# Row sums beside the output, and the last weight piece as two requests, in an attention and soft-MoE kernel

## The chip, the cores and the metric

The kernel runs on one core of a Trainium2 chip. The metric is the device time of one execution in microseconds (us). Five engines work side by side, each through its own queue in order: PE (TensorE: matmuls; PEld, its weight loads, overlap them), DVE (VectorE), ACT (ScalarE), POOL (GpSimd) and SP (SyncE, which here only issues transfers). The data itself is moved by 16 DMA engines. PE writes its results to PSUM, and ACT and DVE evict them to SBUF.

## What is computed

Causal attention with 16 extra "beacon" keys in front gives tokens x, and a soft mixture of experts runs over all tokens. In the reference, cut to what matters:

```python
x = attn_out.transpose(0, 2, 1, 3).reshape(B * S, H * D)      # 4608 x 512
logits = x @ phi                                              # 4608 x 32 slots
d = np.exp(logits - logits.max(0)); d /= d.sum(0) + 1e-09     # over the tokens
slot_input = (d.T @ x).reshape(E, S_per_e, D)                 # 8 experts, 4 slots each
for e in range(E):
    slot_out[e] = np.maximum(slot_input[e] @ w1[e], 0.0) @ w2[e]
c = np.exp(logits - logits.max(1)); c /= c.sum(1) + 1e-09     # over the slots
return c @ slot_out                                           # 4608 x 512
```

B = 8 batches, H = 8 heads, S = 576 tokens, D = 64; w1 is 8 x 512 x 1024, w2 8 x 1024 x 512. No maximum is subtracted in the kernel's fast path: exp of the logits is taken as it is, and a range test at the end, the flag, decides whether a general path has to run after it.

## The kernel before

**Attention.** The main loop (L746 to L783) runs over 32 pairs of heads. For each it computes scores, exponentials, the weighted values and the normalization, and, a few pairs later, transposes x, computes logits and adds each batch's share to the slot inputs (`dispatch`). The exponentials of the logits, transposed, are kept in `eT` (128 x 4608, f16): the 32 slots' rows stand four times over, one below the other. The order of work on every engine is the order in which the program writes it (`manual_schedule`, L666).

**Weights.** `load_weights` (L442) takes 512 KB pieces (f16 as stored; f32 is read and cast on the way) from the list `wchunks` and issues each from POOL's queue. The last in the list is expert 7's second-layer weight, second half (chunks c = 4 to 7), in a tile named `wt`. L786 issues what is left, after the memset of `siz`.

**The tail (L789 to L867).** The last pair is finished, the last batch's logits and slot inputs are computed; `fill` puts in dummy matmuls between them. Then follow `first(eg, fh)` (first layer of four experts at once, half of its 1024 columns), `turn(eg)` (transposes of the result), and `second(eg, c0, c1)` (second layer; it loops over chunks c, inside over four experts, and accumulates in the PSUM tile `so`). `so1` (L863) is its eviction, scaled.

**Row sums.** The output of a token has to be divided by the sum of its 32 exponentials. `row_sums(bb)` (L659) does nine matmuls of `row_tokens(bb, j)` with a column of ones; bb counts quarters of the 4608 tokens (each 128 x 9; two batches of the reference), called batches below. `row_factors` (L840) adds 1e-9 into `stat` and writes the reciprocals into `rc`, on DVE. All four batches' sums share one PSUM tile with `so` (`rsps`). The order on PE is: sums of batch 0 ahead of the last `dispatch`, batch 1 ahead of `first(0, 0)`, batch 2 ahead of `second(1)`, batch 3 behind so1; the factors of 0 and 1 follow `first(0, 0)`, those of 2 and 3 follow the sums of 3 (L865, L866).

**Output (L869 to L924).** For each batch and each j a matmul (L911, tile `fps`, six PSUM buffers) gives 128 x 512 outputs, evicted alternately by ACT (L916) and DVE (L918), scaled by `rc`, into `osb`; SP issues the transfers (L922), three j at a time (six buffers); the first batch begins with one j, then two. The very first j is evicted in two halves, by ACT and DVE at once.

**Range test.** POOL runs three tests of three instructions each (L884 to L888): of `stat` (all sums, 357 columns), of `so1` and of the slot inputs `sz1`. `judge` (L891), called behind the third batch, takes minima on DVE, a matmul, and writes the flag.

Of the kernel before, what the change touches and what calls it, by code (L numbers as in the profile page):

```python
# [9 lines left out]
FP = mybir.dt.float32  # L10
# [3 lines left out]
AL = mybir.AluOpType  # L14
# [37 lines left out]
NJ = 9  # L52
# [3 lines left out]
SUM_LO = 8.0  # L56
SUM_HI = 60000.0
# [211 lines left out]
def kernel(  # L269
# [12 lines left out]
    nc = tc.nc  # L282
    P = 128
    B, H, S, D = q.shape
    Nb = beacon_k.shape[2]
    E, Dm, F = moe_w1.shape
    NSL = moe_phi.shape[1]
    SPE = NSL // E
    NDC = Dm // P
# [16 lines left out]
    ones32 = const.tile([P, 1], F16, name="ones32")  # L306
# [9 lines left out]
    sz1 = const.tile([P, NDC * NSL], F16, name="sz1")  # L316
# [5 lines left out]
    NST = NPAIR * 2 * NC5  # L322
    stat = const.tile([P, NST + 36 + 1], FP, name="stat")

    rd = const.tile([P, 1], FP, name="rd")
    rc = const.tile([P, 4, NJ], FP, name="rc")
    so1 = const.tile([P, Dm], F16, name="so1")
# [6 lines left out]
    ps_av = es.enter_context(tc.tile_pool(name="ps_av", bufs=1, space=PSUM))  # L334
    ps_tr = es.enter_context(tc.tile_pool(name="ps_tr", bufs=2, space=PSUM))
# [60 lines left out]
    def perm_v(b):  # L396
# [12 lines left out]
        for i in range(2):  # L409
# [4 lines left out]
    wchunks = [(e, m, j) for es_ in ((0, 1, 2, 3), (4,)) for m in range(2)  # L414
               for e in es_ for j in range(2)]
    wchunks += [(e, 0, j) for e in (5, 6, 7) for j in range(2)]
    wchunks += [(e, 1, j) for j in range(2) for e in (5, 6, 7)]
    wtail = {}

    def piece(e, m, j):  # L420

        if e < NRES:
            if m == 0:
                return w1h[e][:, 2 * j:2 * j + 2, :].rearrange("p t f -> p (t f)")
            return w2h[e][:, 4 * j:4 * j + 4, :].rearrange("p c d -> p (c d)")
        if (e, m, j) not in wtail:
            if e == NRES:
                t = stv.tile([P, 2, 2048], F16, name="wv", tag="v", bufs=2)
                for i in range(2):
                    wtail[e, m, i] = t[:, i, :]  # L430
            else:
                t = stq.tile([P, 2048], F16, name="wt", tag="kq"[len(wtail) % 2])
                wtail[e, m, j] = t[:, :]
        return wtail[e, m, j]
# [7 lines left out]
    def load_weights(count):  # L442
        for _ in range(count):
            if not wchunks:
                return
            e, m, j = wchunks.pop(0)
            if m == 0:
                nc.gpsimd.dma_start(
                    out=piece(e, m, j),
                    in_=moe_w1[e, 2 * j * P:2 * (j + 1) * P, :].rearrange("(p t) f -> p (t f)", t=2))  # L450
            else:
                src = moe_w2[e].rearrange("(p c) d -> p c d", c=NFC)
                nc.gpsimd.dma_start(
                    out=piece(e, m, j),
                    in_=src[:, 4 * j:4 * j + 4, :].rearrange("p c d -> p (c d)"))

    qTs = {}

# [187 lines left out]
    def row_tokens(bb, j):  # L646

        return eT[:, 2 * S * bb:2 * S * (bb + 1)].rearrange("s (p j) -> s j p", j=NJ)[:, j, :]

    def fill(count, late=True):  # L650

        pool, tag = (ps_tr, "tr") if late else (ps_av, "av")
        ps = pool.tile([P, 512], FP, name="fill", tag=tag)
        for _ in range(count):
            nc.tensor.matmul(ps[:, :], onesh[:, :], eT[:, 0:512], start=True, stop=True)  # L655

    rsp = {}

    def row_sums(bb):  # L659
        if bb == 0:  # L660
            rsp[0] = ps_av.tile([P, 2, 512], FP, name="rsps", tag="av")
        for j in range(NJ):
            nc.tensor.matmul(rsp[0][:, 1, bb * NJ + j:bb * NJ + j + 1], row_tokens(bb, j),
                             ones32[:, :], start=True, stop=True)

    with tc.manual_schedule(engines={ET.PE, ET.DVE, ET.Activation, ET.Pool, ET.SP}):  # L666
        load_qk(0, 0, first=True)
# [2 lines left out]
                          in_=beacon_k.rearrange("b h n d -> (b h) (n d)"))  # L670
# [44 lines left out]
        for c in range(4):  # L715
            for t in range(4):
                nc.vector.tensor_copy(
                    out=sel[32 * c:32 * c + 32, t, :].rearrange(
                        "p (m t) -> p m t", t=4)[:, :, t],
                    in_=idh[32 * c:32 * c + 32, 32 * c:32 * c + 32])  # L720
# [25 lines left out]
        for n in range(2, NPAIR):  # L746
            b, g = divmod(n, NG)
# [46 lines left out]
        normalize(n - 1)  # L794
        x_transposes(n - 2)
        dispatch(B - 2)
        fill(1)
        x_transposes(n - 1)
        logits(B - 1, 0, NDC - 1)
        logits(B - 1, NDC - 1, NDC)  # L800
        row_sums(0)
        sp = dispatch(B - 1, sizv)
        nc.gpsimd.tensor_copy(
            out=sz1[:, :].rearrange("p (t e s) -> p t e s", t=NDC, s=SPE), in_=sizv)
# [29 lines left out]
                        start=(eg == 0 and c == 0),  # L834
                        stop=(eg == E // 4 - 1 and c == NFC - 1))

        rsv = stat[:, NST:NST + 36]
        rcf = rc[:, :, :].rearrange("p a j -> p (a j)")

        def row_factors(j0, j1):  # L840
            nc.vector.tensor_scalar(out=rsv[:, j0:j1], in0=rsp[0][:, 1, j0:j1], scalar1=1e-9,  # L841
                                    scalar2=None, op0=AL.add)
            nc.vector.reciprocal(out=rcf[:, j0:j1], in_=rsv[:, j0:j1])

        row_sums(1)
        first(0, 0)
        row_factors(0, 2 * NJ)
        first(0, 1)
        slot_sums(B - 1, sp, sizv)
        nc.vector.tensor_scalar(out=rd[:, :], in0=stat[:, NST + 36:], scalar1=0.0625e-9,  # L850
                                scalar2=None, op0=AL.add)
# [2 lines left out]
        turn(0)  # L854
        first(1, 1)
        combine_T(B - 1)
        so = rsp[0][:, 0, :]
        second(0, 0, NFC // 2)
        turn(1)
        second(0, NFC // 2)  # L860
        row_sums(2)
        second(1)
        nc.vector.tensor_scalar(out=so1[:, :], in0=so, scalar1=rd[:, 0:1], scalar2=None,  # L863
                                op0=AL.mult)
        row_sums(3)  # L865
        row_factors(2 * NJ, 4 * NJ)  # L866
        es.close()  # L867

        m3 = fast.enter_context(tc.tile_pool(name="m3", bufs=6))  # L869
# [5 lines left out]
        ps_g = fast.enter_context(tc.tile_pool(name="ps_g", bufs=1, space=PSUM))  # L875
# [1 line left out]
        gm = gd.tile([P, 1], FP, name="gm")  # L877
        goodh = gd.tile([P, 1], F16, name="goodh")
        tests = []
        for src, w, low in ((stat, NST + 36 + 1, SUM_LO), (so1, Dm, -SUM_HI),  # L880
                            (sz1, NDC * NSL, -SUM_HI)):
            lo = gd.tile([P, w], FP, name="lo", tag=f"lo{w}")
            hi = gd.tile([P, w], FP, name="hi", tag=f"hi{w}")
            nc.gpsimd.tensor_scalar(out=lo[:, :], in0=src[:, :], scalar1=low, scalar2=None,  # L884
                                    op0=AL.is_ge)
            nc.gpsimd.tensor_scalar(out=hi[:, :], in0=src[:, :], scalar1=SUM_HI, scalar2=None,
                                    op0=AL.is_le)
            nc.gpsimd.tensor_tensor(out=lo[:, :], in0=lo[:, :], in1=hi[:, :], op=AL.mult)  # L888
            tests.append(lo)

        def judge():  # L891
            for i, lo in enumerate(tests):
                nc.vector.tensor_reduce(out=good[:, i:i + 1], in_=lo[:, :], axis=AX.X, op=AL.min)
            nc.vector.tensor_tensor(out=gm[:, :], in0=good[:, 0:1], in1=good[:, 1:2], op=AL.mult)
            nc.vector.tensor_tensor(out=goodh[:, :], in0=gm[:, :], in1=good[:, 2:3], op=AL.mult)
            gp_ = ps_g.tile([1, 1], FP, name="gps")
            nc.tensor.matmul(gp_[:, :], goodh[:, :], onesh[:, 0:1], start=True, stop=True)
            nc.vector.tensor_scalar(out=flag[:, :], in0=gp_[:, :], scalar1=P - 0.5, scalar2=None,
                                    op0=AL.is_lt)
# [3 lines left out]
        for bb in range(4):  # L903
            for (j0, j1) in JS if bb else [(0, 1), (1, 3)] + JS[1:]:
                osb = m3.tile([P, 3, Dm], FP, name="osb", tag="osb")
                for j in range(j0, j1):
                    hw = Dm // 2 if cnt == 0 else Dm
                    fp_ = [ps_f.tile([P, Dm], FP, name="fps", tag="fps")
                           for _ in range(Dm // hw)]
                    for i, f in enumerate(fp_):  # L910
                        nc.tensor.matmul(f[:, 0:hw], row_tokens(bb, j),  # L911
                                         so1[:, hw * i:hw * i + hw], start=True, stop=True)
                    for i, f in enumerate(fp_):
                        ou = osb[:, j - j0, hw * i:hw * i + hw]
                        if (cnt + i) % 2 == 0:
                            nc.scalar.activation(ou, f[:, 0:hw], AF.Copy, scale=rc[:, bb, j:j + 1])  # L916
                        else:
                            nc.vector.tensor_scalar(out=ou, in0=f[:, 0:hw],  # L918
                                                    scalar1=rc[:, bb, j:j + 1], scalar2=None,
                                                    op0=AL.mult)  # L920
                    cnt += 1
                nc.sync.dma_start(out=outr[bb, :, j0:j1, :], in_=osb[:, 0:j1 - j0, :])  # L922
            if bb == 2:
                judge()  # L924
    fast.close()
# [34 lines left out]
```

## Time and profile before

| what | value |
|---|---|
| median of 3 runs (lowest, highest) | 203.09 us (202.74, 204.77) |
| the profiled execution's own time | 203.09 us |
| its span, first to last instruction | 201.4 us |
| busy: PE, DVE, ACT, POOL | 163.2, 132.2, 133.9, 113.9 us |
| moved by the 16 DMA engines | 55.90 MB, mean 278 GB/s |
| mean granted TensorE clock | 0.950 |

How to read the lines further below. On the page, each digit of an engine's line is its busy share, in tenths, of one of 40 equal slices of the span; a queue's line gives packets, MB and the share of 16 engines' span that its packets took. A line of the chain of waits or of the timeline starts with start and length in us; then come the engine, the tile or the operation, and the line of the program; in brackets stands how long the engine had been idle, and what ended that. "SPq", "POOLq" and "DVEq" are those engines' sequencers. A line of a stretch gives its bounds and length, then the busy time (and instructions) of PE, PEld, DVE, ACT and POOL, the granted PE clock, the DMA share and GB/s.

### The profile page before, as it was taken

How to read it: one execution, taken by the hardware profiler on the slowest of the kernel's cores; microseconds unless marked ns; L12 is line 12 of the kernel's file. 1: busy time of each engine (PE TensorE's matmuls, PEld its weight loads, DVE VectorE, ACT ScalarE, POOL GpSimd, SP SyncE). 2: the span in 40 equal slices, each digit the busy share in tenths (PEclk: the TensorE clock that was granted, in tenths of full speed). 3: DMA queues.
4: the chain of work that ended last, by engine and by line, in shares of the span. 5: the costliest groups of instructions: out<-in, count | busy, mean ns of one | idle time of the engine just before them, and what ended most of it. 6: DMA issues, size and time to landing. Idle time of an engine off the chain costs nothing.

```text
span 201.4 us, 7361 instructions
## 1 busy us (share of the span) xinstructions
PE 163.2 (81%) x3121; PEld 107.9 (54%) x3121; DVE 132.2 (66%) x275; ACT 133.9 (66%) x172; POOL 113.9 (57%) x263
## 2 busy tenths in 40 slices
PE   6798893889889898988988899898989997966200
PEld 2433661668567476666756667675767753522000
DVE  0352784688987888887887878878837332898300
ACT  2355784689878888889887788987895230774200
POOL 6049186469649757865965786898786000890000
PEclk9999999799999999999999999999999999995855
DMA  6999999999999999999999999999999991499991
GB/s 206 254 244 365 278 361 317 270 370 311 267 271 378 264 261 349 292 275 305 356 232 279 379 273 268 264 219 217 211 216 212 213 202 30 176 410 417 408 405 78
DMA packets 29701, 55.90 MB, mean 278 GB/s; under 512 B 7228, under 2 KB 15644, under 8 KB 29660
## 3 DMA queue, kind: packets, MB, share of 16 engines
q1 hardware_dynamic: 24764, 37.98, 55.4%
q0 software_dynamic: 4608, 16.78, 41.7%
q10 hardware_dynamic: 288, 0.59, 1.0%
q8 instruction: 26, 0.43, 0.8%
q14 instruction: 15, 0.12, 0.2%
HBM read 62.69 MB, written 9.44 MB: 358 GB/s over the span
## 4 chain that ended last, share of the span: by engine, by line
PE 60%; DMA 10%; ACT 9%; DVE 8%; POOL 3%; issue 3%; SPq 0%; ACTq 0%; DVEq 0%; POOLq 0%
PE sc L514 15%; PE av L535 15%; PE trps L483 9%; DMA wt<-in_moe_w_dram 7%; ACT expT L519 5%; PE xtps L561 5%; DVE osb L918 4%; ACT vh L407 4%; PE vpt L404 2%; DMA kstag<-in_k_dram 2%; PE fill L655 2%; PE fps L911 2%; PE lgps L580 2%; PE vps L404 2%; PE sips L619 2%
## 5 line engine op out<-in xcount | busy, mean ns | idle before, releaser
L519 ACT ACTIVATE expT<-sc 128x992 f16<-128x992 f32 (+3 forms) x128 | 104.8, 867 | 20.6 <-PE sc L514 20.0
L505 POOL TENSOR_SCALAR_AFFINE_SELECT expT<-expT 128x224 f16<-128x224 f16 (+3 forms) x128 | 54.9, 439 | 40.1 <-ACT expT L519 39.2
L514 PE MATMUL sc<-qT,kT 64*128 64x80 bf16 (+4 forms) x576 | 43.8, 246 | 10.8 <-ACT expT L519 5.5
L535 PE MATMUL av<-vh,expT 128*128 128x65 f16 (+1 forms) x960 | 40.4, 195 | 0.4 <-DVE x L549 0.2
L535 PEld LDWEIGHTS <-expT 128*128 128x128 f16 (+1 forms) x960 | 33.7, 98 | 4.5 <-POOL expT L505 0.6
L495 DVE COPY kT<-trps 128x640 bf16<-128x640 bf16 (+1 forms) x31 | 22.7, 773 | 19.8 <-PE trps L483 19.3
L514 PEld LDWEIGHTS <-kT 64*128 64x128 bf16 x576 | 17.0, 95 | 28.1 <-issue 22.2
L495 DVE COPY qT<-trps 128x640 bf16<-128x640 bf16 (+1 forms) x30 | 22.0, 774 | 8.2 <-PE trps L483 6.3
L549 DVE TENSOR_TENSOR x<-av,r 128x640 f16<-128x640 f32 x32 | 26.4, 825 | 1.1
L390 POOL CAST vc<-vstag 128x512 f16<-128x512 f32 x32 | 18.6, 611 | 1.8 <-DMA vstag<-in_beacon_v_dram 1.8
L916 ACT ACTIVATE osb<-fps,rc 128x512 f32<-128x512 f32 (+1 forms) x18 | 11.0, 678 | 12.2 <-PE fps L911 10.9
L568 DVE COPY xT<-xtps 128x576 f16<-128x576 f16 x31 | 14.2, 457 | 6.5 <-PE xtps L561 6.5
L561 PE MATMUL xtps<-idh,x 128*128 128x128 f16 (+2 forms) x160 | 14.1, 216 | 1.1 <-issue 1.0
L918 DVE TENSOR_SCALAR osb<-fps,rc 128x512 f32<-128x512 f32 (+1 forms) x19 | 12.8, 731 | 1.3 <-PE fps L911 1.1
L655 PE MATMUL fill<-eT,onesh 128*128 128x512 f16 x35 | 11.4, 453 | 1.7 <-POOL onesh L684 1.5
L407 ACT ACTIVATE vh<-vps 128x1024 f16<-128x1024 f32 x8 | 8.2, 1027 | 6.6 <-PE vpt L404 6.6
L561 PEld LDWEIGHTS <-x 128*128 128x128 f16 (+2 forms) x160 | 9.0, 97 | 6.6 <-issue 6.0
L410 DVE CAST vh<-vpt 128x512 f16<-128x512 f32 x16 | 10.3, 685 | 3.4 <-PE vpt L404 3.4
L911 PE MATMUL fps<-so,eT 128*128 128x512 f16 (+1 forms) x37 | 11.6, 433 | 0.5 <-DVE stat L841 0.3
L462 POOL COPY kT<-bkA 64x32 bf16<-64x32 bf16 x32 | 7.4, 231 | 7.9 <-DVE bkA L712 6.9
L483 PE MATMUL trps<-idb,kstag 128*64 128x128 bf16 x270 | 11.6, 234 | 0.1
L483 PE MATMUL trps<-idb,qstag 128*64 128x128 bf16 x270 | 10.7, 222 | 0.5 <-DVE vh L410 0.4
(98 smaller groups left out, 186.7 us busy)
## 6 DMA issues: line engine op xcount, KB each, us to landing
kstag<-in_k_dram SPq DMA_DIRECT2D x15, 576.0 KB, 9.4
qstag<-in_q_dram SPq DMA_DIRECT2D x15, 576.0 KB, 13.4
out_dram<-osb SPq DMA_DIRECT2D x11, 768.0 KB, 7.6
vstag<-in_v_dram SPq DMA_DIRECT2D x7, 1024.0 KB, 15.3
w1h<-in_moe_w_dram POOLq DMA_DIRECT2D x10, 512.0 KB, 8.6
w2h<-in_moe_w_dram POOLq DMA_DIRECT2D x10, 512.0 KB, 8.5
wt<-in_moe_w_dram POOLq DMA_DIRECT2D x8, 512.0 KB, 12.2
wv<-in_moe_w_dram POOLq DMA_DIRECT2D x4, 512.0 KB, 11.6
```

Of the source, the lines that this page charges most:

```text
L390: nc.gpsimd.tensor_copy(out=st["c", b][:, :, hs, :].rearrange("p t h d -> p h t d"), in_=st["v", b][:, hs, :, :])
L407: nc.scalar.activation(vhs[b % 2][:, 0:2, :, 0:D], ps[:, :, :].rearrange("p c (h d) -> p c h d", d=D), AF.Copy)
L483: nc.tensor.transpose(tp[lo:hi, j - j0, :], t[:, hh, j, :].bitcast(BF)[:, 1::2], idb[:, :])
L495: nc.vector.tensor_copy(out=do, in_=ti)
L505: nc.gpsimd.affine_select(out=ap, in_=ap, compare_op=AL.is_ge, fill=0.0, base=cbase, pattern=pat, channel_multiplier=-1)
L514: nc.tensor.matmul(sc[:, hh, col:col + qw], kTs[n // 2 % 2][po:po + D, n % 2, c * P:(c + 1) * P], qTs[n // 2][po:po + D, n % 2, q0:q0 + qw ...
L519: nc.scalar.activation(ex[:, :, base:base + w], sc[:, :, 0:w], AF.Exp, scale=scale)
L535: nc.tensor.matmul(av[:, i, :], exps[n % 2][0:KW[c], hh, o:o + P], vhs[b % 2][0:KW[c], c, h, :], start=(c == 0), stop=(c == i))
L549: nc.vector.tensor_tensor(out=xs[b][:, :, head(n, 0):head(n, 1) + 1:head(n, 1) - head(n, 0), :].rearrange("p i h d -> p h i d"), in0=av[:, ...
L561: nc.tensor.transpose(tp[:, QLO[i]:QLO[i] + QW[i]], xs[b][0:QW[i], i, 2 * t:2 * t + 2, :].rearrange("p h d -> p (h d)"), idh[0:QW[i], 0:QW ...
L911: nc.tensor.matmul(f[:, 0:hw], row_tokens(bb, j), so1[:, hw * i:hw * i + hw], start=True, stop=True)
L918: nc.vector.tensor_scalar(out=ou, in0=f[:, 0:hw], scalar1=rc[:, bb, j:j + 1], scalar2=None, op0=AL.mult)
```

## The change

Four edits go together. (1) The last weight piece is issued as two requests of two chunks each. (2) `row_sums` gets its PSUM tile as an argument and does the factors itself, for one batch; batch 0's tile comes from the pool of transposes, batch 1's from that of `av`, and `so` has a tile of its own. (3) The sums of batches 2 and 3 move into the output loop, behind the third request of batch 0 and the second request of batch 1 (j = 3 to 5), with a PSUM tile of the one-buffer pool that the judge's matmul uses too. (4) The test of `stat` moves from the head of POOL's tests into `judge`, so POOL tests `so1` and `sz1` first. A second dummy matmul is added ahead of the last x transposes.

```diff
+    WLAST = wchunks[-1]
...
-                nc.gpsimd.dma_start(
-                    out=piece(e, m, j),
-                    in_=src[:, 4 * j:4 * j + 4, :].rearrange("p c d -> p (c d)"))
+                cs = 2 if (e, m, j) == WLAST else 4
+                for c in range(0, 4, cs):
+                    nc.gpsimd.dma_start(
+                        out=piece(e, m, j)[:, c * Dm:(c + cs) * Dm],
+                        in_=src[:, 4 * j + c:4 * j + c + cs, :].rearrange("p c d -> p (c d)"))
...
-    rsp = {}
-
-    def row_sums(bb):
-        if bb == 0:
-            rsp[0] = ps_av.tile([P, 2, 512], FP, name="rsps", tag="av")
+    rsv = stat[:, NST:NST + 36]
+    rcf = rc[:, :, :].rearrange("p a j -> p (a j)")
+
+    def row_sums(bb, rsp):
+
         for j in range(NJ):
-            nc.tensor.matmul(rsp[0][:, 1, bb * NJ + j:bb * NJ + j + 1], row_tokens(bb, j),
-                             ones32[:, :], start=True, stop=True)
+            nc.tensor.matmul(rsp[:, j:j + 1], row_tokens(bb, j), ones32[:, :], start=True,
+                             stop=True)
+        sl = slice(bb * NJ, bb * NJ + NJ)
+        nc.vector.tensor_scalar(out=rsv[:, sl], in0=rsp[:, 0:NJ], scalar1=1e-9, scalar2=None,
+                                op0=AL.add)
+        nc.vector.reciprocal(out=rcf[:, sl], in_=rsv[:, sl])
...
-        fill(1)
+        fill(2)
...
-        row_sums(0)
+        row_sums(0, ps_tr.tile([P, NJ], FP, name="rsps", tag="tr"))
...
-        row_sums(1)
+        row_sums(1, ps_av.tile([P, 2, 512], FP, name="rsps", tag="av")[:, 0, :])
         first(0, 0)
-        row_factors(0, 2 * NJ)
         first(0, 1)
...
-        so = rsp[0][:, 0, :]
+        so = ps_av.tile([P, 2, 512], FP, name="so", tag="av")[:, 0, :]
         second(0, 0, NFC // 2)
         turn(1)
         second(0, NFC // 2)
-        row_sums(2)
         second(1)
         nc.vector.tensor_scalar(out=so1[:, :], in0=so, scalar1=rd[:, 0:1], scalar2=None,
                                 op0=AL.mult)
-        row_sums(3)
-        row_factors(2 * NJ, 4 * NJ)
...
+        test(so1, Dm, -SUM_HI)
+        test(sz1, NDC * NSL, -SUM_HI)
+
         def judge():
+            test(stat, NST + 36 + 1, SUM_LO)
...
                 nc.sync.dma_start(out=outr[bb, :, j0:j1, :], in_=osb[:, 0:j1 - j0, :])
+                if bb in (0, 1) and j0 == 3:
+                    row_sums(bb + 2, ps_g.tile([P, NJ], FP, name="rsps", tag="g"))
             if bb == 2:
                 judge()
```

More of the change, by code (lines that the diff above doesn't have):

```diff
@@ L835, in second @@
                         stop=(eg == E // 4 - 1 and c == NFC - 1))
[L837 to L843, printed above, removed]
-        row_sums(1)
+        row_sums(1, ps_av.tile([P, 2, 512], FP, name="rsps", tag="av")[:, 0, :])
         first(0, 0)
-        row_factors(0, 2 * NJ)
         first(0, 1)
@@ L879, with test @@
         tests = []
-        for src, w, low in ((stat, NST + 36 + 1, SUM_LO), (so1, Dm, -SUM_HI),
-                            (sz1, NDC * NSL, -SUM_HI)):
+        def test(src, w, low):
             lo = gd.tile([P, w], FP, name="lo", tag=f"lo{w}")
@@ L895, in judge @@
             nc.vector.tensor_tensor(out=goodh[:, :], in0=gm[:, :], in1=good[:, 2:3], op=AL.mult)
-            gp_ = ps_g.tile([1, 1], FP, name="gps")
+            gp_ = ps_g.tile([1, 1], FP, name="gps", tag="g")
             nc.tensor.matmul(gp_[:, :], goodh[:, :], onesh[:, 0:1], start=True, stop=True)
```

## The prediction, made before the result was known

> **What bounds the kernel now.** I read the page first, then the chain of waits, then the transfers second by second around the place where the weights end and the output begins.
>
> ```profile
> span 201.4 us, 7361 instructions
> PE 163.2 (81%) x3121; PEld 107.9 (54%) x3121; DVE 132.2 (66%) x275; ACT 133.9 (66%) x172; POOL 113.9 (57%) x263
> DMA  6999999999999999999999999999999991499991
> q1 hardware_dynamic: 24764, 37.98, 55.4%
> q0 software_dynamic: 4608, 16.78, 41.7%
> ```
>
> No engine is full, but the DMA line is: it stands at 9 in every slice, except at the start, at the end, and in the two slices numbered 1 and 4 (slices of 5.03 us, so 166 to 176 us). The kernel is a stream of transfers with one hole. Ahead of the hole lie the inputs and weights, behind it the output. What shortens the hole shortens the time; what an engine does beside the stream costs nothing until the stream runs dry. The chain of waits, from 160 us on, shows what fills the hole:
>
> ```profile
> 154.15 14.88 DMA wt<-in_moe_w_dram
> ...
> 169.08 1.04 PE rsps L831 x13
> ...
> 170.15 0.76 DVE so L863
> ...
> 170.95 0.66 PE rsps L663 x9
> ...
> 171.63 0.19 DVE stat L841
> ...
> 171.86 0.61 PE fps L911 x3
> ...
> 172.51 0.05 DVEq L918
> ...
> 172.61 3.78 DVE osb L918 x6
> ```
>
> The last weight piece lands at 169.04 (154.15 + 14.88). Then come 13 matmuls of the second layer, its eviction (`so1`), nine row sum matmuls of the last batch, the factors of the last two on VectorE, and only then the first output matmul. The transfers beside it, stretch by stretch (the last two columns are DMA share and GB/s):
>
> ```profile
> 160.00:165.00 5.00, 5.00 (x87) 2.26 (x75) 1.62 (x5) 2.39 (x4) 0.00 (x0) 1.00 1.04 210
> 167.00:168.00 1.00, 1.00 (x22) 0.66 (x24) 0.00 (x0) 0.00 (x0) 0.00 (x0) 1.00 0.17 33
> 168.00:169.00 1.00, 0.52 (x11) 0.02 (x4) 0.00 (x0) 0.00 (x0) 0.00 (x0) 1.00 0.04 8
> 173.00:174.00 1.00, 1.00 (x5) 0.50 (x4) 1.00 (x3) 1.00 (x3) 0.94 (x2) 1.00 0.00 0
> 174.00:175.00 1.00, 0.94 (x4) 0.41 (x3) 1.00 (x3) 1.00 (x2) 0.92 (x2) 1.00 1.01 385
> 183.00:197.00 14.00, 4.15 (x10) 1.40 (x10) 4.04 (x7) 2.75 (x4) 0.00 (x0) 0.62 1.01 405
> 197.00:198.00 1.00, 0.00 (x0) 0.00 (x0) 0.00 (x0) 0.00 (x0) 0.00 (x0) 0.50 0.39 145
> ```
>
> In the last microsecond before the landing the share is 0.04, which is 0.6 of one of 16 DMA engines: a single trailing engine holds up everything. From 174 to 197 us the output transfers run without a gap (share about 1), so the end is the start of the output plus a constant. A profiled execution of 203.09 us with a span of 201.4 is the one that I sum against; its time happens to be the median of the runs as well.
>
> **Part 1, the last weight piece in two requests.** In PE's queue the second layer of experts 4 to 7 runs through the chunks c = 4 to 7 of the last piece in order:
>
> ```profile
> 166.62 0.70 PE L663 MATMUL rsps<-ones,eT 128*128 128x1 f16 x9
> 167.26 0.39 PE L831 MATMUL rsps<-w2h,hT 128*32 128x512 f16 x1
> ...
> 168.14 0.38 PE L831 MATMUL rsps<-wt,hT 128*32 128x512 f16 x1
> 169.08 0.38 PE L831 MATMUL rsps<-wt,hT 128*32 128x512 f16 x1 [0.57 <-DMA wt<-in_moe_w_dram]
> ...
> 169.31 0.38 PE L831 MATMUL rsps<-w2h,hT 128*32 128x512 f16 x1
> ...
> 169.53 0.38 PE L831 MATMUL rsps<-w2h,hT 128*32 128x512 f16 x1
> ```
>
> PE reaches expert 7's chunk 4 at 168.51 (169.08 less 0.57) and waits. With the row sums of batch 2 gone from here (166.62 to 167.26, 0.64) it gets there at 167.87. The first half should have landed by then: at 210 GB/s a 512 KB piece takes 2.5 us, a half 1.25, so about 167.8. Chunks 4 and 5 then run inside the wait; a chunk is 0.22 (169.31 to 169.53). PE stands before chunk 6 at 168.3 and waits there. Behind the wait are left 1.04 - 2 x 0.22 = 0.60 us instead of 1.04: **-0.44**, if the second half lands when the whole did.
>
> The price of one more request appears in no row by itself. From below it is 0: through 160 to 165 us requests of this queue follow one another at share 1.04, without a gap between them. From above: 16 packets of half the size in place of 8 on the trailing engine, if a packet cost the same whatever its size. A packet of this queue takes 0.417 x 16 x 201.4 / 4608 = 0.29 us, so 8 more are 2.3 us. But the other hardware queue, with 1.5 KB a packet, takes 0.072 us for each, that is 47 ns a KB against 80 ns a KB here, where two bytes are read for each that is written: the time goes by bytes. I take +0.1, near the lower end. **Sum of part 1: -0.34.**
>
> The request also costs its issue on POOL:
>
> ```profile
> 154.15 0.55 POOL L453 DMA_DIRECT2D wt<-in_moe_w_dram  x1 [0.15 <-issue]
> 154.69 1.08 POOL L785 MEMSET siz<- 128x1152 f16 x1
> 159.00 0.29 POOL L803 COPY sz<-siz 128x128 f16<-128x128 f16 x1 [3.23 <-DVE siz L622]
> ```
>
> 0.55 us more put the memset's end at 156.3; the tile is filled by VectorE (L622) shortly before it releases POOL at 159.0, so over 2 us are left. Nothing. The second request enters 14 us ahead of its landing, behind a backlog.
>
> **Part 2, batches 2 and 3's sums behind the output's start.** Today so1 ends and row sums follow at 170.95; the first output matmul starts at 171.86, released by the factor (L841). With the sums and their factors gone, that matmul takes the slot at 170.95: **-0.91**. It needs so1 and a PSUM buffer whose last reader is now so1's eviction itself.
>
> **Part 3, VectorE's queue.** The first output tile is evicted in two halves, one on ACT and one on VectorE.
>
> ```profile
> 171.84 0.27 DVE L843 RECIPROCAL rc<-stat 128x18 f32<-128x18 f32 x1
> 171.86 0.38 PE L911 MATMUL fps<-so,eT 128*128 128x256 f16 x2 [0.27 <-DVE stat L841]
> 172.22 0.47 ACT L916 ACTIVATE osb<-fps,rc 128x256 f32<-128x256 f32 x1 [7.84 <-PE fps L911]
> 172.61 0.48 DVE L918 TENSOR_SCALAR osb<-fps,rc 128x256 f32<-128x256 f32 x1 [0.50 <-PE fps L911]
> L918 DVEq EVENT_SEMAPHORE  x8: 21/50/50, 171.9 to 172.5; - x8
> 173.17 0.36 SPq L922 DMA_DIRECT2D out_dram<-osb  x1
> ```
>
> Both matmuls are done at 172.24. VectorE starts at 172.61 because eight semaphore steps stand in its queue from 171.9 to 172.5. They began as soon as the reciprocal was issued, so they run under an instruction. In the new order so1, 0.75 us long, stands ahead of them and covers them. ACT began 0.09 after its matmul's end (172.13 to 172.22); with that, VectorE begins at 172.33: **-0.28**. Bounds: 0, if one of the steps waits for something late, and -0.39, ACT's own start. The first request (173.17) waits for this half, so it moves along.
>
> **Part 4, what is put into the output phase.** Twice nine row sum matmuls (0.70 on PE) and twice an add and a reciprocal (0.18 + 0.27 by the wider rows, on VectorE), after tiles 3 to 5 of batches 0 and 1. What hides them is the lead of the evictions over the transfers:
>
> ```profile
> 175.15 0.33 SPq L922 DMA_DIRECT2D out_dram<-osb  x1
> 175.80 0.33 SPq L922 DMA_DIRECT2D out_dram<-osb  x1
> ```
>
> A tile of 256 KB takes 0.64 us at 405 GB/s. The three requests up to 175.15 carry six tiles, so they last from 174.0 to 177.9. The next request goes out at 175.80; the first one needed 0.83 from issue to flow (173.17 to 174.0), so it has 177.9 - 176.6 = 1.3 us in hand, and 0.45 on VectorE or 0.70 on PE fits. If that cover were gone, up to 0.7 would be paid once. Later the lead is larger, since the evictions wait for free output buffers.
>
> POOL's test of the sums, three instructions of at most 1.13 each, moves behind the third batch. VectorE's three minima then wait for it, with the last batch's VectorE evictions queued behind them:
>
> ```profile
> 171.90 1.13 POOL L884 TENSOR_SCALAR lo<-stat 128x357 f32<-128x357 f32 x1 [12.62 <-DVE stat L841]
> ...
> 181.57 1.30 DVE L893 TENSOR_REDUCE good<-lo 128x1 f32<-128x357 f32 x3
> 188.19 0.35 SPq L922 DMA_DIRECT2D out_dram<-osb  x1
> ```
>
> The last request is issued at 188.19 and the stream runs dry only after 197, so some 8 us of backlog cover even a wait for all of it. Nothing. The other edits lie ahead of the weights' landing, where PE now has 0.85 us to spare (168.3 to about 169.15): one more filler matmul, 0.38 by the rows of 512 columns, and batch 0's add and reciprocal ahead of the slot inputs on VectorE, 0.45 if nothing covers them. Together 0.83, which fits. Nothing, unless the second half lands earlier.
>
> **Sum:** -0.34 - 0.91 - 0.28 = -1.53, so 203.09 - 1.53 = **201.56 us**.
>
> **The rivals.** *A: the halves travel singly.* If the second half started only when the first had landed at 167.8, it would need 0.83 to start, 1.25 to move and 0.4 to complete (one engine at share 0.04 x 16 stops near 168.64, the landing is at 169.04): 170.28, 1.24 late. Then 203.09 - 0.44 + 1.24 - 0.91 - 0.28 = 202.7. For it: the two are separate requests. Against it: share 1.04 through the two pieces that 160 to 165 us hold (5 us at 210 GB/s). The Trainium skill, "DMA: Bandwidth & Descriptors", section "Anatomy of one DMA — SWDGE (gpsimd) path", states a fixed cost of about 2.0 us for each DMA, mostly completion; charged in full to the second request, an estimate by that page, the time would be 203.5. The gapless share above speaks against charging it to a request that is queued behind another.
>
> *B, the other side: packets cost by number.* At the upper bound of part 1 the trailing engine ends 2.3 us later: 203.09 - 0.44 + 2.3 - 0.91 - 0.28 = 203.8. It decides from 1.63 us on, where the three gains are eaten; for over 1% slower, 3.7 us would be needed. Against it stands the cost by bytes.
>
> *C: the trailing engine trails less.* If its delay belongs to this execution, or two requests spread it, the landing moves to where PE stands ready, 168.3: up to 0.75 more, and 203.09 - 1.53 - 0.75 = 200.8.
>
> *D: the edit does nothing,* because the output's end is set otherwise. Against it: no gap in the stream from 174 to 197. It would give 203.1.
>
> **How the numbers follow.** A measurement of this kernel can tell about 1% (2.03 us) from no change; so faster means under 201.06, slower over 205.12. Forecast 0.60 (its own range 201.0 to 202.2), A 0.13, B 0.09, C 0.11, D and the rest 0.07. The range 200.8 to 203.2 takes in the forecast, A, C and D, and leaves out B and the extremes. Faster by over 1%: C and a little of the forecast, 0.17. Slower by over 1%: a worse B, or a stall that no row prices, 0.08. Within 1%: 0.75.
>
> **What the new profile would show.** Part 1: PE's wait for the weight piece now before its last 5 or so matmuls of L831, and 0.6 us from landing to so1. Part 2: the first fps matmul some 0.05 us after so1. Part 3: VectorE's first osb within 0.15 us of ACT's. Part 4: DMA share near 1 from the output's first byte on. I am wrong if the weights land over 0.5 us later or earlier than 169.04, if the output stream shows a gap around the new row sums, or if its length differs by more than 0.5 us.

## The result, and the profile after

| kernel | median (lowest, highest), 22 executions each | ratio, 95% interval |
|---|---|---|
| before, in the same group | 204.51 us (202.69, 206.63) | |
| changed | 201.63 us (200.31, 203.9) | 0.9885 (0.9855 to 0.9914) |

The ratio leaves out executions over 1.5% above the fastest of their kernel (3 and 4 of 22 here), so it is not the ratio of the medians, and it shifts with that one fastest execution: in the first group of the experiments, where the kernel before has one at 201.79, 15 of its 36 fall out. It says 1.15% faster, 2.35 us of 204.51. Forecast were 1.53 us, to 201.56. The level fits better than the difference: the kernel before stands 1.4 us higher in this group than in the three executions that the forecast started from, and the medians lie 1.35 us further apart than forecast. That the two cancel is luck. A second group, further below, gave 0.9919 (0.9881 to 0.9957).

The page of the changed kernel, two of the lines shown of before:

```profile
span 198.9 us, 7368 instructions
DMA  6999999999999999999999999999999995599991
```

The hole in the stream is still in the same two slices, but smaller (5 and 5 tenths instead of 1 and 4; a slice is now 4.97 us). The stretches of transfers, the DMA share and GB/s last:

```profile
167.00:168.00 1.00, 1.00 (x23) 0.35 (x16) 0.00 (x0) 0.00 (x0) 0.00 (x0) 1.00 0.17 31
168.00:169.00 1.00, 0.76 (x8) 0.24 (x5) 0.18 (x1) 0.00 (x0) 0.00 (x0) 1.00 0.00 0
171.00:172.00 1.00, 1.00 (x13) 0.85 (x12) 1.00 (x3) 0.86 (x3) 1.00 (x2) 1.00 0.48 180
180.00:194.00 14.00, 3.94 (x10) 1.42 (x10) 4.98 (x11) 2.75 (x4) 0.00 (x0) 0.67 1.02 409
```

The weights end before 168 (before: after 168.6), and the output flows from 171.5 (before: 174.0). The chain of waits has no pieces in this execution; the timeline shows what lies between:

```profile
167.79 0.77 PE L838 MATMUL so<-wt,hT 128*32 128x512 f16 x2
168.19 0.39 PE L838 MATMUL so<-w2h,hT 128*32 128x512 f16 x1
...
168.82 0.75 DVE L860 TENSOR_SCALAR so<-so,rd 128x512 f16<-128x512 f32 x1 [2.40 <-PE so L838]
169.62 0.38 PE L909 MATMUL fps<-so,eT 128*128 128x256 f16 x2 [0.84 <-DVE so L860]
169.98 0.47 ACT L914 ACTIVATE osb<-fps,rc 128x256 f32<-128x256 f32 x1 [5.63 <-PE fps L909]
170.10 0.48 DVE L916 TENSOR_SCALAR osb<-fps,rc 128x256 f32<-128x256 f32 x1 [0.53 <-PE fps L909]
170.66 0.36 SPq L920 DMA_DIRECT2D out_dram<-osb  x1
```

The wait for the weights now stands within chunk 6, the group from 167.79 on: its two `wt` matmuls end 0.77 us after they began, where two without a wait take 0.38; chunk 7 follows at 168.19. The first output matmul stands 0.05 us behind so1's end, and VectorE's first osb 0.12 behind ACT's. These are the pictures that the forecast asked for. The first request went out 2.51 us earlier (170.66 for 173.17).

The points of the path in all profiles of this study, in us of each execution's own span. The weights' end is the end of the last packet of their queue in the trace, the first output byte the start of the first packet of the other queue behind it.

| kernel | median (before beside it) | slot inputs written | weights' end | so1 starts | first output matmul | first output byte | output stream, length |
|---|---|---|---|---|---|---|---|
| before | 204.51 | 158.64 | 168.73 | 170.15 | 171.86 | 174.03 | 24.79 |
| before again | 204.04 (204.24) | 158.35 | 168.64 | 170.04 | 171.76 | 173.92 | 24.81 |
| sums in a tile of their own | 203.09 (203.76) | 159.81 | 169.12 | 170.54 | 171.34 | 173.58 | 24.77 |
| two requests alone * | 204.66 (204.24) | 161.16 | 169.84 | 173.39 | 175.10 | 177.27 | 24.79 |
| two dummies alone * | 205.32 (203.84) | 159.57 | 169.09 | 171.68 | 173.40 | 175.56 | 24.81 |
| changed | 201.63 (204.51) | 158.63 | 167.83 | 168.82 | 169.62 | 171.51 | 24.82 |
| changed again * | 202.32 (203.84) | 160.75 | 170.05 | 172.01 | 172.82 | 174.71 | 24.78 |
| changed, one request * | 202.66 (204.24) | 159.40 | 169.25 | 170.77 | 171.58 | 173.47 | 24.86 |
| changed, four requests | 202.15 (204.24) | 158.38 | 168.20 | 168.98 | 169.79 | 171.68 | 24.81 |
| changed, one dummy | 201.95 (203.84) | 160.01 | 169.05 | 170.01 | 170.82 | 172.71 | 24.83 |
| changed, VectorE behind so1 | 202.12 (203.76) | 160.52 | 170.32 | 171.28 | 172.08 | 173.97 | 24.82 |
| changed, sums first | 203.22 (203.76) | 161.28 | 170.29 | 171.25 | 172.05 | 173.95 | 25.52 |
| changed, sums four times | 206.97 (203.76) | 159.46 | 168.94 | 169.91 | 170.72 | 172.61 | 28.40 |
| changed, four requests, so1 halved * | 202.48 (203.84) | 160.22 | 169.93 | 171.53 | 172.57 | 174.46 | 24.77 |

(* PE's clock is halved there for 3.4 us from about 160 us on; more of that below.)

Before against changed: the slot inputs come at the same time (158.64, 158.63), so1 1.33 earlier, the first matmul 0.91 and the first byte 0.27 more. Of the 1.33, 0.90 are the weights' end and 0.43 what lies behind it. The output streams are equally long. So every term of the sum is there in its size, and 0.9 us stand beside it that the forecast had only in a rival (C, 0.75). An end of the weights more than 0.5 us off was one of the forecast's own signs of being wrong.

### The profile page after: what moved, and what is told of

The parts are those of the page before. It is cut to its first block, busy times and chain, and to the rows that moved or that the text cites. A ratio compares the mean times of both kernels' runs of the same rounds, so it can differ in the third digit from the quotient of the medians.

```text
span 198.9 us, 7368 instructions
## 1 busy us (share of the span) xinstructions
PE 162.4 (82%) x3122; PEld 107.9 (54%) x3122; DVE 132.4 (67%) x279; ACT 134.0 (67%) x172; POOL 114.8 (58%) x264
## 4 chain that ended last, share of the span: by engine, by line
## 5 line engine op out<-in xcount | busy, mean ns | idle before, releaser
L410 DVE CAST vh<-vpt 128x512 f16<-128x512 f32 x16 | 10.3, 684 | 3.6 <-PE vpt L404 3.6
```

## The experiments

Theory 1: the terms of the sum are all there is, and the 0.9 us are scatter of the weights' stream between executions. Theory 2: two requests shorten the trail of the slowest DMA engine. Theory 3, formed on the way: the second dummy matmul keeps PE's clock up.

**Two requests alone,** on the kernel before:

```diff
+    WLAST = wchunks[-1]
...
+                cs = 2 if (e, m, j) == WLAST else 4
+                for c in range(0, 4, cs):
+                    nc.gpsimd.dma_start(
...
```

> Only edit 1 on the kernel before: the last weight piece in two requests. Theory 1 (the halves only let chunks 4 and 5 run inside the wait; the 0.9 us by which the weights landed earlier in the changed kernel's profile is scatter between executions): 0.44 less work behind the landing and about 0.1 for the request, but the row sums of batch 2 still stand ahead of chunk 4, so PE reaches chunk 6 at about 168.95 instead of 168.3; the time falls by 0.3, ratio 0.998 to 0.999. Theory 2 (two requests shorten the trail of the slowest DMA engine): the weights land near 168.2 and the wait vanishes; so1 starts 1.0 to 1.3 earlier than the 170.15 of before, ratio 0.993 to 0.995.

Measured: 204.66 beside 204.24, ratio 1.0054 (1.0012 to 1.0097): no gain. The unchanged kernel, below, has the same ratio, so this is not a loss either. In its profile PE's clock is halved from 161.5 on, PE reaches the second layer after the weights have landed, and so1 starts 3.55 behind their end. There the halves can't matter. Between the theories its time tells nothing.

**One request in the changed kernel.**

```diff
-                cs = 2 if (e, m, j) == WLAST else 4
+                cs = 4
```

> The changed kernel with the last weight piece whole again, as one request; edits 2 to 4 stay. Theory 1: 0.34 us more than the changed kernel, 1.2 less than before by the moved sums and VectorE's queue; with the same scatter, ratio to before 0.990 to 0.994. Theory 2: the weights land near 169.0 to 169.1 again; ratio to before 0.994 (1.2 us), and the changed kernel lies 1.3 us below this one.

Measured: 202.66 beside 204.24, 1.58 less by the medians; ratio 0.9986 (0.9942 to 1.0029). The two readings differ by more than a microsecond. But the unchanged kernel has a ratio of 1.0051 in this group; against that, 0.9986 is 0.994, or 1.3 us. Both theories expected 1.2 here, so the run agrees with a gain of the moved sums and does not part the theories. Its profile too has the halved clock.

**Four requests.**

```diff
-                cs = 2 if (e, m, j) == WLAST else 4
+                cs = 1 if (e, m, j) == WLAST else 4
```

> The changed kernel with the last weight piece in four requests of one chunk each. Behind the landing of the last chunk only about 0.38 us of matmuls are left instead of 0.60. Theory 1: up to 0.22 less than the changed kernel, less two more requests at 0 to 0.1 each, so equal to it within 0.2. Theory 2: the landing moves earlier once more, by up to 0.5, but PE reaches the last chunk only at about 168.0, so no more than 0.4 less. If packets cost by their number, the weights land over 1 us later.

Measured: 202.15 beside 204.24, ratio 0.9960 (0.9924 to 0.9997), which is 0.991 against the unchanged kernel of this group: not distinguishable from two requests. From the weights' end to so1 it is 0.78 us, as expected 0.2 less than with two. The waits are now at the last two chunks: within chunk 6, whose `wt` matmuls end 0.77 after their start, and before the last matmul of chunk 7:

```profile
167.52 0.77 PE L838 MATMUL so<-wt,hT 128*32 128x512 f16 x2
167.92 0.39 PE L838 MATMUL so<-w2h,hT 128*32 128x512 f16 x1
...
168.57 0.38 PE L838 MATMUL so<-wt,hT 128*32 128x512 f16 x1 [0.25 <-DMA wt<-in_moe_w_dram]
```

**Before, unchanged.**

> The kernel before, unchanged, for the scatter of the weights' landing and of the ratio. Theory 1: the landing lies anywhere from 168.2 to 169.5 against 169.04 in the profile shown; ratio 1 within 0.004. Theory 2: the landing lies within 0.3 of 169.04.

Measured: 204.04 beside 204.24, yet ratio 1.0051 (1.0006 to 1.0096), for one and the same kernel. The medians agree; what lifts the ratio is the choice of executions told with the result. So the ratios of this group (this run, two requests alone, one request, four requests) read half a percent too high, and ratios of different groups can't be compared to 0.5%. That is why the table counts by points of the path.

**Sums of batches 2 and 3 in a tile of their own,** still ahead of the output, on the kernel before:

```diff
+        if bb == 2:
+            rsp[2] = ps_tr.tile([P, 4 * NJ], FP, name="rsps2", tag="tr")
+        rs = rsp[0][:, 1, :] if bb < 2 else rsp[2]
...
```

> The kernel before, with the row sums of batches 2 and 3 still ahead of the output, but in a PSUM tile of their own instead of the one that the second layer uses. In the kernel before the sums of batch 3 began 0.05 us after so1's end (170.95), although they read nothing of so1. If they waited only because of the shared tile, they now run under so1 (0.66 us under 0.75), and VectorE's add follows so1 at once: the first output matmul starts about 0.25 us after so1's end (still released by the add) instead of 0.95, 0.7 of the 0.91 of part 2. If it was their place that cost, the first output matmul still starts 0.9 us after so1's end.

Measured: ratio 0.9968 (0.9929 to 1.0007). The timeline:

```profile
170.43 0.70 PE L666 MATMUL rsps<-ones,eT 128*128 128x1 f16 x9
170.54 0.75 DVE L867 TENSOR_SCALAR so<-rsps,rd 128x512 f16<-128x512 f32 x1 [2.93 <-PE rsps L834]
171.20 0.17 DVE L845 TENSOR_SCALAR stat<-rsps 128x18 f32<-128x18 f32 x1
171.34 0.27 PE L915 MATMUL fps<-so,eT 128*128 128x256 f16 x1 [0.21 <-DVE so L867]
...
172.17 0.48 DVE L922 TENSOR_SCALAR osb<-fps,rc 128x256 f32<-128x256 f32 x1 [0.50 <-ACT osb L920]
```

The row sums run under so1, and the first output matmul starts 0.05 us behind so1, released by so1 and no longer by the add. That is all of the 0.91 of part 2, more than the 0.7 that I expected. The sums of batch 3 had waited only because they were written into the tile that so1 was read from. Their place costs no more than what is still missing here: the first byte comes 3.04 us behind so1's start, against 3.88 before and 2.69 in the changed kernel, because VectorE has the add, the reciprocal and its eight semaphore steps ahead of its first osb, which starts 0.48 behind ACT's.

**A VectorE instruction more behind so1.**

```diff
+        nc.vector.reciprocal(out=rcf[:, 0:2 * NJ], in_=rsv[:, 0:2 * NJ])
         es.close()
```

> The changed kernel with one VectorE instruction more behind so1: batch 0 and 1's reciprocals once more, into the same place (the same values). It takes 0.27 us itself. If part 3 is right, the eight semaphore steps of VectorE's queue begin only when it is issued, at so1's end, and VectorE's first osb starts 0.4 us after ACT's again (0.12 in the changed kernel); the first output request goes out 0.28 later. If the steps do not hang on what stands ahead of them, VectorE starts at most 0.15 after ACT. The time rises by 0.3 or by nothing; the profile tells which.

Measured, in four executions: 202.12 beside 203.76, ratio 0.9885 (0.9827 to 0.9943). The timeline of VectorE and ACT:

```profile
171.28 0.75 DVE L860 TENSOR_SCALAR so<-so,rd 128x512 f16<-128x512 f32 x1 [2.97 <-PE so L838]
171.95 0.26 DVE L862 RECIPROCAL rc<-stat 128x18 f32<-128x18 f32 x1
...
172.44 0.47 ACT L915 ACTIVATE osb<-fps,rc 128x256 f32<-128x256 f32 x1 [6.20 <-PE fps L910]
172.56 0.48 DVE L917 TENSOR_SCALAR osb<-fps,rc 128x256 f32<-128x256 f32 x1 [0.36 <-PE fps L910]
```

And the view of the output's line, with VectorE's semaphore steps (count, shortest, median and longest in ns, first and last start):

```profile
L917 DVEq EVENT_SEMAPHORE  x8: 50/50/367, 171.3 to 172.3; - x8
```

The semaphore steps began at 171.3, with so1, although the reciprocal stands ahead of them; VectorE is 0.12 behind ACT as without it. So six of the eight do not hang on what is executed ahead of them. The longest, 367 ns, ended at 172.25, just behind the reciprocal, and cost nothing, since the first output matmul was still running (172.08 and 0.38). In the kernel before, the reciprocal that stood there itself had to wait for the add; this one waits for nothing.

**The sums first,** behind the first and second request of batch 0:

```diff
-                if bb in (0, 1) and j0 == 3:
-                    row_sums(bb + 2, ps_g.tile([P, NJ], FP, name="rsps", tag="g"))
+                if bb == 0 and j0 in (0, 1):
+                    row_sums(j0 + 2, ps_g.tile([P, NJ], FP, name="rsps", tag="g"))
```

> The changed kernel with both late row sums right behind the first two output requests (one tile, then two) of batch 0, where the evictions have no lead over the transfers yet. If the lead is what hides them: VectorE's next eviction comes 0.4 us later for each, and the transfers run dry for 0.4 to 1.0 us around the second and third request; the output stream ends that much later. If anything in the output phase is free: no gap, and the length of the output stream is that of the changed kernel (24.8 us from first byte to last).

Measured: ratio 0.9957 (0.9927 to 0.9988); the output stream is 25.52 us long, 0.70 more. The stretches show both holes (share and GB/s last):

```profile
174.00:174.50 0.50, 1.00 1.02 389
174.50:175.00 0.50, 1.00 0.29 107
...
176.00:176.50 0.50, 1.00 0.54 213
```

The lead of the evictions is what hides the sums at their own place.

**The sums four times over.**

```diff
+                    for _ in range(4):
-                    row_sums(bb + 2, ps_g.tile([P, NJ], FP, name="rsps", tag="g"))
+                        row_sums(bb + 2, ps_g.tile([P, NJ], FP, name="rsps", tag="g"))
```

> The changed kernel with each of the two late row sums done four times over at its place (the same result each time). One takes 0.64 on PE and 0.4 on VectorE, and with one PSUM buffer the four follow one another: about 1.1 us each, 4.4 in all, against 1.1 once. By part 4 the lead there is 1.3 us, so about 2 us of the first block are not hidden: the DMA share falls near 175 to 177 us and the stream ends 1.5 to 2.5 later; the second block stands where evictions wait for buffers and is hidden in part. If the lead is larger than I think (over 4 us), nothing changes.

Measured, in four executions: ratio 1.014 (1.0089 to 1.0191); the stream is 28.40 us long, 3.58 more than the changed kernel's.

```profile
174.68 0.64 PE L666 MATMUL rsps<-ones,eT 128*128 128x1 f16 x9 [0.26 <-DVE stat L669]
...
175.58 0.65 PE L666 MATMUL rsps<-ones,eT 128*128 128x1 f16 x9 [0.26 <-DVE stat L669]
```

```profile
176.00:177.00 1.00, 0.50 0.50 197
177.00:179.00 2.00, 0.50 0.00 0
179.00:180.00 1.00, 1.00 0.93 387
```

A round takes 0.90 us, so three more make the first block 2.7 longer, where I had 3.3; 2.5 us of stream are lost there and about 1 at the second block (share 0.78 and 0.20 from 184 to 186 us), which I had thought better covered. PE's clock is halved from 175.6 on as well, which slows the matmuls behind the block, so not all of the 3.58 is the sums' own. A lead of over 4 us is ruled out; its exact size can't be read from this run.

**The changed kernel with one dummy matmul, the changed kernel again, and the kernel before with two dummies:**

```diff
-        fill(2)
+        fill(1)
```

> The changed kernel with one dummy matmul ahead of the last x transposes instead of two. Two runs so far (one request with two dummy matmuls, two requests in the kernel before with one) show PE's clock halved for one window near 160 us, in the first layer of the experts, and there PE reaches the second layer after the weights have landed. Theory 3 (the second dummy matmul makes that window rarer, and is worth what the sum does not explain): 0.6 to 0.9 us more than the changed kernel, a lower mean clock. Theory 1 (it costs nothing and gives nothing; the windows come at random): equal to the changed kernel within 0.4.

> The changed kernel once more, as the measure for the others of this group, and for the gap between the 1.53 of the sum and the 2.4 us measured. Theory 1 (scatter of where the weights' stream stands): the difference of the medians to before lies between 1.2 and 2.4, and the weights land anywhere between 167.8 and 170.5. Theory 2 (two requests shorten the trail, always): the landing lies within 0.4 of 168.1 and the difference is 2.4 again.

> The kernel before with two dummy matmuls ahead of the last x transposes instead of one, nothing else. Theory 3: 0.6 to 0.9 us less than before, ratio 0.996. Theory 1: equal to before within 0.4, since PE waits for the weights 0.6 us anyhow and one such matmul takes 0.22 to 0.38.

Measured beside 203.84: one dummy 201.95, ratio 0.9935 (0.9895 to 0.9975); changed again 202.32, ratio 0.9919 (0.9881 to 0.9957); before with two 205.32, ratio 1.0038 (0.9999 to 1.0076). Theory 3 has fallen: the dummy matmul gains nothing on either kernel, and the last two profiles have the halved window in spite of it. The changed kernel's gain in this group is 1.52 by the medians and 1.65 by the ratio. Its weights ended at 170.05, not near 168.1; but its slot inputs came 2.1 us later too, and from them to the weights' end it is 9.3 us, for 9.2 in the first profile.

**Four requests, and so1 halved between VectorE and ACT:**

```diff
+        nc.vector.tensor_scalar(out=so1[:, 0:Dm // 2], in0=so[:, 0:Dm // 2], scalar1=rd[:, 0:1],
+                                scalar2=None, op0=AL.mult)
+        nc.scalar.activation(so1[:, Dm // 2:Dm], so[:, Dm // 2:Dm], AF.Copy, scale=rd[:, 0:1])
```

> A version that could beat both: the changed kernel with the last weight piece in four requests, and so1 evicted in halves, columns 0 to 255 on VectorE and 256 to 511 on ACT. If the chain landing, second layer, so1, first output matmul sets the start of the output: 0.2 less behind the landing than the changed kernel (0.78 instead of 0.97, as the run with four requests showed), and 0.27 less for so1 (0.48 instead of 0.75, by the 256-column eviction of the output); 0.45 us less than the changed kernel in all. If VectorE's eight semaphore steps (0.7 us) now outlast so1's half, VectorE's first osb is late again by 0.25 and half of it is lost.

Measured: 202.48 beside 203.84, ratio 0.9928 (0.9888 to 0.9968): no better than the changed kernel. The halves run one after the other:

```profile
171.53 0.48 DVE L860 TENSOR_SCALAR so<-so,rd 128x256 f16<-128x256 f32 x1 [2.05 <-PE so L838]
172.05 0.47 ACT L862 ACTIVATE so<-so,rd 128x256 f16<-128x256 f32 x1 [4.64 <-DVE so L860]
172.57 1.46 PE L910 MATMUL fps<-so,eT 128*128 128x256 f16 x7 [1.13 <-ACT so L862]
```

ACT waited for VectorE, though each reads and writes columns of its own, and so1 took 1.04 to the first matmul instead of 0.80. Both halves lie in one PSUM bank. The Trainium skill, "PSUM — Partial Sum Buffer", section "PSUM bank collisions raise a hardware error", says that two engines may not read one bank in the same partitions at once, and that software therefore orders them. The wait above agrees. That both write into one SBUF tile is not what orders them: the two halves of the first osb do so too, from two PSUM tiles, and overlap (169.98 and 170.10 in the changed kernel, each 0.47 or 0.48 long). A PSUM tile over two banks was not tried.

## Why the prediction was right, and where it was not

**Part 1 (-0.44, price +0.1).** Right in size where PE waits for the weights: from their end to so1 it is 1.40 to 1.42 us with one request (before, before again, own tile), 0.96 to 0.99 with two (changed, one dummy, VectorE behind so1, sums first, sums four times) and 0.78 with four. The extra request's price is not seen: from the slot inputs to the weights' end it is 9.8 us in the mean with one request (five profiles, 9.3 to 10.3), 9.2 with two (seven, 8.7 to 9.8) and 9.8 with four (two). Rivals A and B, and charging the second request in full with the 2.0 us that the prediction took from the Trainium skill, are thereby out. But two and four requests do not lie in an order, so Theory 2 isn't shown. Nor do the packets of the weights' queue settle it: from the last moment with eight of them in flight to the end of the last it is 0.8 to 1.7 us with one request, 0.3 to 1.3 with two, 0.6 and 1.0 with four. Whether two requests make the weights land 0.5 earlier stays open.

**Part 2 (-0.91).** Right in size. The reason was incomplete: I let the whole gain come from the sums' new place. The run with a tile of its own shows the 0.91 without the move.

**Part 3 (-0.28; measured 0.27).** Right in size, with a reason that was too narrow. The steps do run under so1, as forecast, but it need not be the last instruction ahead of them; what held them before was an instruction that waited. The run with the added reciprocal shows the first of these. That the wait held them is read from the profiles of before and own tile, and wasn't tried by itself.

**Part 4 (nothing).** Right: the stream's length is 24.82 for 24.79, and it grows by 0.70 where there is no lead. The test of the sums and judge's wait cost nothing either, by the same length.

**What the sum left out.** It was made for an execution in which PE waits for the weights. Five of the 14 profiles are not like that: PE's clock is halved from about 160 us on, in the experts' first layer. Then the second layer is PE's own chain, and what counts is the row sums of batch 2, taken out of it. From the slot inputs to so1, with these sums between:

```profile
159.57 0.29 DVE L622 SCALAR_TENSOR_TENSOR siz<-sips,acc 128x128 f16<-128x128 f32 x1 [0.46 <-PE sips L619]
...
169.09 0.70 PE L663 MATMUL rsps<-ones,eT 128*128 128x1 f16 x9
...
171.68 0.75 DVE L863 TENSOR_SCALAR so<-rsps,rd 128x512 f16<-128x512 f32 x1 [2.77 <-PE rsps L831]
```

```profile
160.75 0.29 DVE L625 SCALAR_TENSOR_TENSOR siz<-sips,acc 128x128 f16<-128x128 f32 x1
172.01 0.75 DVE L860 TENSOR_SCALAR so<-so,rd 128x512 f16<-128x512 f32 x1 [2.03 <-PE so L838]
```

Above the kernel before (with two dummies), 12.11 us; below the changed kernel again, 11.26. Of the 0.85 between them some 0.75 lie behind the start of the second layer, where the sums stood, and 0.1 ahead of it, in the first layer. The other two changed kernels with the halved clock, with one and with four requests, have 11.37 and 11.31, so the number of requests does not matter there. With parts 2 and 3 the gain is 1.93 there, against 1.63 where PE waits. At five to nine the mean would be 1.7. The two groups gave 2.35 and 1.65 by their ratios, with intervals of 1.76 to 2.97 and 0.88 to 2.43 us: 1.7 lies within the second and at the edge of the first. What the first group gained beyond it, and the 0.9 us in its profile, can be scatter of the weights' stream or Theory 2; no run here parts them. The step of the prediction that fell short is the sentence that took row sums 2 ahead of the second layer only as slack: taking them out is a gain of its own whenever the slack is gone.

## What to carry to other kernels

Read a wait by what it waits for, not by what stands there: two results in one tile tie their readers and writers together, and a tile of its own gave the same 0.91 us as moving the work. Where a stream of transfers is the bound, extra work is free only as far as the producers lead; reckon that lead in us at the very place (here 1.3), since 0.70 were paid at the head of the stream. And one profile is one execution: a sum made on it holds for the waits that it happened to have, so look at several profiles before taking a term as slack.

## What was not expected of the hardware

Executions of one kernel differ by 2 us and more, and with them differs how often PE's clock is halved: for one to four windows of 3.4 us between 20 and 46 us, and sometimes once more near 160. One early window came with slot inputs at 158.35 to 158.64 (before, before again, changed, four requests), two to four with 159.4 to 161.3. The stretches of the kernel before, then of the changed kernel again (clock, DMA share and GB/s last):

```profile
20.00:46.00 26.00, 20.42 (x426) 0.93 1.05 321
160.00:164.00 4.00, 4.00 (x70) 1.00 1.06 214
```

```profile
20.00:46.00 26.00, 20.58 (x366) 0.80 1.06 318
160.00:164.00 4.00, 4.00 (x59) 0.58 1.06 213
```

Whether the extra window comes can be read from where the windows lie. In each profile the clock changes on a grid of 3.41 us. Continued from the first change behind 20 us, the grid has a line between 0.1 us ahead of the slot inputs and 0.8 us behind them in just the five profiles with the extra window, and the window begins at that line; in the other nine the nearest lines are 0.67 us or more ahead and 2.0 us or more behind.

The Trainium skill, "TensorE: Matmul & The Clock Gate", section "What's actually happening", has a window of 3413 ns that runs freely and does not start anew with a kernel; the lengths and the grid here agree. That the clock falls after an idle window, as it says too, does not agree: with one request in the changed kernel PE was busy 2.82 of the 3 us from 157 to 160, and the clock fell at 160.2:

```profile
157.00:160.00 3.00, 2.82 (x71) 1.00 1.06 212
160.00:163.00 3.00, 3.00 (x34) 0.53 1.05 213
```

A packet of the cast weights took 324 ns for 4096 bytes written, 173 ns for 2048 and 98 ns for 1024 in the traces, so the time goes by bytes, with some 22 ns for the packet itself.
